# A list scheduler with other durations, a model of the TensorE clock, and due times shifted by kind in five stretches

## The chip, the cores and the metric

The kernel runs on one core of one Trainium2 chip. The metric is the device time of one execution in microseconds (us). The core has five engines with a queue each: TensorE (PE in the profile; its weight loads are PEld), VectorE (DVE), ScalarE (ACT), GpSimd (POOL) and SyncE (SP), which issues most DMAs.

## The reference

Two layers, one after the other, in float32. The first is a linear attention with a decaying state (4 batches, 8 heads, 768 steps, head size 48); the second a feed-forward net whose hidden layer is the maximum of three products. Cut to what matters:

```python
for t in range(S):                                   # S = 768
    cur = einsum('bhd,bhe->bhde', u[None] * k_t, v_t)
    y[:, :, t] = einsum('bhd,bhde->bhe', r_t, state + cur)
    state = w[None, :, :, None] * state + einsum('bhd,bhe->bhde', k_t, v_t)
x = y.transpose(0, 2, 1, 3).reshape(B * S, H * D)    # 3072 tokens x 384
h = maximum(maximum(x @ w1, x @ w2), x @ w3)         # 3072 x 768
out = h @ w_out                                      # 3072 x 384
```

## The kernel before

**Tiling.** The 768 steps are cut into 12 chunks of 64. A chunk holds 64 steps of 4 batches, that is 256 tokens, and each chunk is worked in two halves q of four heads. Within a chunk the recurrence is turned into matrix products: scores of r against k, a mask that keeps earlier steps, scores against v, and r against the state that earlier chunks left. Products are made from pairs of float16 numbers (a high and a low part) in three matmuls; chunk 0 uses float32 matmuls instead.

**Pieces of one chunk.** Loads from DRAM of `feat` (k and r, steps along the free dimension) and `tok` (k, r, v, steps along partitions). DVE or, from chunk 3, POOL scales them by powers of the decay (`kT`, `rT`, `kdec`) and makes the diagonal (`am`). ACT makes high parts (`kdh`, `rh`, `ah`, `ktdh`, `vdh`, `sdh`), DVE low parts (`kdl`, `rl`, `al`, `ktdl`, `vdl`, `sdl`). SP then copies kd, ktd, vd and sd block by block into kb, ktb, vb and sb by DMAs within the chip (`spread`, lines 308 to 310, two DMAs each). PE does `sc` (24 matmuls a half), `va` (48) and `ke` (24); `ke` leads to the next state. ACT and DVE take `va` out of PSUM as `xh` and `xl` (lines 456 and 461), the inputs of the feed-forward part. There PE does 18 `up` products of 9 matmuls each; the maximum is taken as they leave PSUM (ACT `m` at line 502, then DVE `m` twice at line 506); `hh` (ACT) and `hl` (POOL or DVE) are the parts of the result; three `dn` products of 18 matmuls give the output, which ACT takes out (`io`) and stores. ACT also sums squares of all inputs, of the state, of x and of the weights (`sq`, `xsq`, `wsq`; "junk" at lines 252 and 340), which DVE tests at the end (`check`, `good`, `flag`); the fallback behind the test isn't taken here.

**Weights** come once, in 16 pieces (`word`), as 64-bit numbers that ACT and DVE turn into float16 pairs: `ztop` (ACT), `word` (DVE), `his` (ACT), `lo` (DVE). Four buffers hold pieces that are under way.

**Order.** Nothing is ordered by hand line by line. A planner in the kernel's own Python (`Plan`, line 40) gets each piece with an engine, an expected duration, what it reads and writes, the buffers it takes and a due time in units of chunks. `order` (line 86) plays the pieces forward: of the pieces that could start first on an engine it takes the one with the smallest due time. The instructions are then written in the order of the planned starts, so every engine and the SP queue work through a fixed list, in order, and wait at its head whatever stands behind. A plan's times are never used on the chip, only its order.

**Due times.** Each piece's due time is its chunk plus an offset, plus a shift looked up by kind, such as `"act sq"`. Before, a kind has two shifts: one for due times up to `OPENING` = 1.6 and one behind. A transfer is expected to take its bytes by `RATE`, in one pipe, 1.5 us behind its issue, and to be seen 0.9 us after it ends. Kinds that stand next to GpSimd work are stretched (`near`). PE's pieces have one duration whatever its clock; chunk 0's are written at a slow clock (3.65 us for its `sc`).

Of the kernel before, what the change touches and what calls it, by code (L numbers as in the profile page):

```python
# [38 lines left out]

class Plan:  # L40

    LAG = {"pe": 0.25, "dve": 0.1, "act": 0.2, "pool": 0.15}
    ISSUE = {"sp": 0.45, "act": 0.45, "pool": 1.0}
    RATE, BEFORE, BEHIND = 275e3, 1.5, 0.9
    OPENING = 1.6
    SHIFT = {
        "act ah": (-5.31, -0.9), "act am": (2.08, 0), "act hh": (1.37, 0.4), "act his": (-0.69, 0), "act io": (-5.36, -2.55),
        "act kb": (-1.33, 0), "act kdh": (-2.9, 1.2), "act ktb": (1.56, 0), "act ktdh": (2.65, 0.45), "act m": (0.81, -0.9),  # L50
        "act odd": (0, 0.6), "act rh": (1.04, -0.85), "act sdh": (-5.26, 2.75), "act sq": (-6.83, 0.2), "act state": (-3.36, 0),
        "act tkt": (-0.31, 0), "act vb": (-2.77, 0), "act vdh": (-3.65, 2.05), "act xh": (1.12, -1.45), "act ztop": (-4.35, 0),
        "dve a": (4.95, 2.4), "dve al": (5.58, 0.7), "dve am": (-3.84, 0.85), "dve ends": (0, 0.45), "dve flag": (0, -2),
        "dve good": (0, -3), "dve hl": (2.63, -2.25), "dve kT": (6.29, 0), "dve kdec": (8.61, 0), "dve kdl": (-1.52, -0.15),
        "dve ktdl": (-3.55, 1.1), "dve lo": (-4.52, 0), "dve m": (-2.24, 0.3), "dve rT": (9.32, 0), "dve rl": (-2.27, 0.75),
        "dve sdl": (3.31, -0.15), "dve state": (-2.75, 1.5), "dve vdl": (4.98, 0.55), "dve vet": (0, -0.15), "dve word": (-1.81, 0),
# [10 lines left out]
    def do(self, due, eng, cost, fn, reads=(), writes=(), takes=(), size=0, near=0):  # L67
# [16 lines left out]
        self.todo.append(dict(n=n, due=due, eng=eng, cost=cost, fn=fn, need=need, takes=takes, size=size, near=near, kind=kind, late=late, touch={*reads, *writes, *new}))  # L84

    def order(self, free):

        free, pipe = dict(free), 0.0
# [14 lines left out]
        def earliest(p):  # L103
            t = free[p["eng"]]
            for m in p["need"]:
                q = self.todo[m]
                t = max(t, end[m] if q["eng"] != p["eng"] or q["size"] and not p["size"] else start[m] + busy[m] + (0 if p["size"] else 0.06))
# [7 lines left out]
            return t  # L115

        while ready:
# [30 lines left out]
        self.when = start  # L148
        return [self.todo[n] for n in sorted(out, key=lambda n: start[n])]
# [3 lines left out]
def kernel(ctx, tc, feat, tok, wu, ut, ws, wo, cst, out):  # L153
# [518 lines left out]
    def dma(due, fn, size, reads=(), writes=(), takes=(), eng="sp", n=1):  # L672
        do(due, eng, n * Plan.ISSUE[eng], fn, reads, writes, takes, size)
# [34 lines left out]
    def before_scores(c, q, due):
# [7 lines left out]
        dma(due - 0.22, lambda: spread(nc.sync, kb, kd, C), 524288, reads=["kdh", "kdl"], writes=["kb"], n=2)  # L716
# [13 lines left out]
    def before_keys(c, q, due):  # L730
# [5 lines left out]
        dma(due - 0.20, lambda: spread(nc.sync, ktb, ktd, C), 524288, reads=["ktdh", "ktdl"], writes=["ktb"], n=2)  # L736

    def before_values(c, q, due):
# [3 lines left out]
        dma(due - 0.22, lambda: spread(nc.sync, vb[q], vd[q], D), 393216, reads=[vh, vl], writes=[("vb", q)], n=2)  # L742

    def first_scores(q, due):
# [6 lines left out]
        do(due, "pe", 3.65, lambda: full("sc", q, kb, C, P, units(raws[c, q]["rT"])), reads=[f, "kb", ("rT", c, q)], takes=[("psa", ("sc", c, q))])  # L751
        do(due + 0.02, "dve", dve(U * C), lambda: mask(c, q), reads=[("sc", c, q)], writes=[("am", c, q)])

    def first_values(q, due):
        c = 0
        do(due, "pe", 2.8, lambda: full("va", q, vb[q], C, R, raws[c, q]["a"]), reads=[("am", c, q), ("vb", q)], writes=[("xq", 0)] * q, takes=[("psa", ("va", c, q))])
        leave_x(c, q, due)

    def first_keys(q, due):
# [3 lines left out]
        do(due, "pe", 3.2, lambda: full("ke", q, ktb, D, C + D, units(raws[c, q]["v"])), reads=["ktb", t], takes=[("psa", ("ke", c, q))])  # L763
# [13 lines left out]
    def after_keys(c, q, due):  # L777
# [17 lines left out]
    def leave_x(c, q, due):  # L795
# [12 lines left out]
        if q:  # L808
            do(due + 0.9, "act", act(NJ * TOK) + 0.1, lambda: x_sum(c, T["x", c][0]), reads=[hi], writes=[("xsq", c)])
# [19 lines left out]
    def ffn(c):  # L829
# [30 lines left out]
        def part(m, fs, due):  # L860
# [14 lines left out]
    do(-0.55, "pe", 1.1, turn, takes=[("psa", "turned")])  # L875
# [5 lines left out]
    do(-0.45, "pe", 2.2, stir, reads=[("xq", 0)], writes=["stirred"], takes=[("psm", "stir")])  # L881
# [15 lines left out]
    do(4.9, "dve", 1.2, check_ends, reads=[("begun", 4)], writes=["ends"])  # L897
    do(NCH - 0.4, "dve", 1.5, check, reads=["ends", *(k for k in plan.wrote if k[0] in ("sq", "xsq", "wsq"))], writes=["good"])
# [67 lines left out]
```

## Time and profile before

| | |
|---|---|
| median of 3 runs | 405.27 us (403.41, 405.27, 408.9) |
| the profiled execution's own time | 405.38 us |
| its span, first to last instruction | 403.5 us |
| mean granted TensorE clock | 0.983 |
| busy PE, PEld, DVE, ACT, POOL | 372.7, 334.0, 276.7, 265.1, 182.2 us |
| moved by DMA | 80.69 MB, mean 200 GB/s |

An engine's busy time is the time in which it executed something; ends of matmuls are modelled, so that a busy PE may still run at half its clock. A row of instructions gives its start, its length, engine, line, operation, out<-in, shapes, how many it merges, and in brackets the idle time before it with who ended it. SPq and ACTq are queues that issue DMAs.

### The profile page before, as it was taken

How to read it: one execution, taken by the hardware profiler on the slowest of the kernel's cores; microseconds unless marked ns; L12 is line 12 of the kernel's file. 1: busy time of each engine (PE TensorE's matmuls, PEld its weight loads, DVE VectorE, ACT ScalarE, POOL GpSimd, SP SyncE). 2: the span in 40 equal slices, each digit the busy share in tenths (PEclk: the TensorE clock that was granted, in tenths of full speed). 3: DMA queues.
4: the chain of work that ended last, by engine and by line, in shares of the span. 5: the costliest groups of instructions: out<-in, count | busy, mean ns of one | idle time of the engine just before them, and what ended most of it. 6: DMA issues, size and time to landing. Idle time of an engine off the chain costs nothing.

```text
span 403.5 us, 11979 instructions
## 1 busy us (share of the span) xinstructions
PE 372.7 (92%) x4768; PEld 334.0 (83%) x4768; DVE 276.7 (69%) x540; ACT 265.1 (66%) x698; POOL 182.2 (45%) x180
## 2 busy tenths in 40 slices
PE   2879788998999799999899999999999999999995
PEld 2877677887888589989789989999899989999784
DVE  6889889974859786695766865875876865443420
ACT  5989979695747755764764854765766784844421
POOL 9100000059655579658268378368557633010110
PEclk9998899999999789999999999999999999999999
DMA  8899787999399999859588688788887963500001
GB/s 288 310 326 257 200 238 213 280 286 263 107 247 244 292 264 255 214 166 255 138 262 232 151 247 240 191 216 217 235 209 202 268 162 88 147 2 15 27 2 45
DMA packets 28655, 80.69 MB, mean 200 GB/s; under 512 B 4528, under 2 KB 9392, under 8 KB 28592
## 3 DMA queue, kind: packets, MB, share of 16 engines
q1 hardware_dynamic: 23264, 75.03, 67.4%
q10 hardware_dynamic: 5328, 4.82, 3.8%
q8 instruction: 39, 0.64, 0.7%
q14 instruction: 24, 0.20, 0.2%
HBM read 36.41 MB, written 4.72 MB: 102 GB/s over the span
## 4 chain that ended last, share of the span: by engine, by line
PE 43%; DMA 16%; ACT 8%; DVE 6%; issue 3%; ACTq 1%; SPq 1%; POOL 0%; DVEq 0%
PE psm L487 36%; PE psa L400 7%; DMA kb<-kd 6%; DMA tok<-in_tok_dram 4%; DMA feat<-in_feat_dram 3%; DMA ktb<-ktd 3%; ACT xh L456 2%; ACT junk L340 1%; ACTq L867 1%; ACT junk L252 1%; DVE m L506 1%; DVE ktd L327 1%; ACT kd L322 1%; ACT rh L362 1%; ACT io L532 1%
## 5 line engine op out<-in xcount | busy, mean ns | idle before, releaser
L487 PEld LDWEIGHTS <-w 128*128 128x128 f16 x2592 | 252.2, 99 | 45.3 <-issue 14.4
L487 PE MATMUL psm<-xh,w 128*128 128x256 f16 x1296 | 226.3, 276 | 5.4 <-ACT m L502 2.7
L487 PE MATMUL psm<-xl,w 128*128 128x256 f16 x648 | 156.1, 276 | 5.3 <-DVE xl L461 4.9
L515 POOL TENSOR_TENSOR hl<-m,hh 128x256 f16<-128x256 f32 x55 | 45.6, 830 | 148.5 <-ACT hh L509 74.6
L506 DVE SCALAR_TENSOR_TENSOR m<-psm,m 128x256 f32<-128x256 f32 x144 | 60.1, 419 | 63.8 <-PE psm L487 37.5
L509 ACT CAST hh<-m 128x256 f16<-128x256 f32 x72 | 28.8, 401 | 64.0 <-DVE m L506 63.4
L487 PE MATMUL psm<-hh,w 128*128 128x256 f16 x432 | 55.7, 273 | 0.0
L357 POOL TENSOR_TENSOR feat<-feat,wrt 128x512 f32<-128x512 f32 x36 | 50.2, 1409 | 4.4 <-DMA feat<-in_feat_dram 4.4
L340 ACT ACTIVATE junk<-tok 128x384 bf16<-128x384 f32 x72 | 37.3, 518 | 14.5 <-DMA tok<-in_tok_dram 13.0
L376 POOL TENSOR_TENSOR am<-tok,u_sb 128x384 f32<-128x384 f32 x18 | 21.3, 1183 | 46.5 <-DVE al L420 32.6
L461 DVE SCALAR_TENSOR_TENSOR xl<-psa,xh 32x256 f16<-32x256 f32 (+2 forms) x60 | 28.2, 471 | 16.3 <-ACT xh L456 15.2
L502 ACT ACTIVATE m<-psm 128x256 f32<-128x256 f32 x72 | 27.1, 378 | 14.2 <-PE psm L487 10.5
L487 PE MATMUL psm<-hl,w 128*128 128x256 f16 x216 | 33.5, 273 | 0.7 <-POOL hl L515 0.7
L400 PE MATMUL psa<-ah,vb 128*128 128x64 f16 x352 | 33.9, 195 | 0.0
L400 PE MATMUL psa<-rh,sb 128*128 128x64 f16 x352 | 33.5, 195 | 0.0
L400 PE MATMUL psa<-al,vb 128*128 128x64 f16 x176 | 31.7, 195 | 0.6 <-DVE al L420 0.6
L400 PE MATMUL psa<-rl,sb 128*128 128x64 f16 x176 | 31.7, 195 | 0.0
L400 PEld LDWEIGHTS <-vb 128*128 128x128 f16 x528 | 29.8, 100 | 1.4 <-issue 0.8
L327 DVE TENSOR_TENSOR kd<-feat,kd 128x512 f16<-128x512 f32 x22 | 20.8, 944 | 13.1 <-ACT kd L322 12.6
L400 PEld LDWEIGHTS <-sb 128*128 128x128 f16 x528 | 28.1, 99 | 0.0
L456 ACT ACTIVATE xh<-psa 32x256 f16<-32x256 f32 (+2 forms) x60 | 24.9, 414 | 2.0 <-PE psa L400 1.2
L390 POOL TENSOR_TENSOR am<-cs,a 128x512 f32<-128x512 f32 x18 | 21.1, 1174 | 7.2 <-DVE a L381 7.2
(96 smaller groups left out, 550.0 us busy)
## 6 DMA issues: line engine op xcount, KB each, us to landing
tok<-in_tok_dram SPq DMA_DIRECT2D x24, 576.0 KB, 6.9
feat<-in_feat_dram SPq DMA_DIRECT2D x24, 512.0 KB, 5.3
raw<-in_ws_dram SPq DMA_DIRECT2D x12, 576.0 KB, 7.5
kb<-kd SPq DMA_DIRECT2D x22, 256.0 KB, 5.8
kb<-kd SPq DMA_DIRECT2D x22, 248.0 KB, 6.2
ktb<-ktd SPq DMA_DIRECT2D x20, 256.0 KB, 3.4
ktb<-ktd SPq DMA_DIRECT2D x20, 248.0 KB, 4.2
out_dram<-io ACTq DMA_DIRECT2D x36, 128.0 KB, 5.0
```

Of the source, the lines that this page charges most:

```text
L327: nc.vector.tensor_tensor(out=dense.dense[:, 1, :, 0:w], in0=src, in1=dense.dense[:, 0, :, 0:w], op=ALU.subtract)
L340: nc.scalar.activation(out=junk[:, 0:U * D].rearrange("p (u d) -> p u d", u=U), in_=src, func=AF.Square, scale=scale, accum_out=stat[:, ki ...
L357: helper(c).tensor_tensor(out=t[n], in0=t[n], in1=tb, op=ALU.mult)
L376: helper(c).tensor_tensor(out=w.rearrange("p (g b) d -> p g b d", g=2), in0=t["r"], in1=by_token(u_sb, q), op=ALU.mult)
L400: nc.tensor.matmul(out=ps, lhsT=l[i], rhs=rr[j], start=first and n == 0, stop=last and n == 2)
L456: nc.scalar.mul(out=hi, in_=src, mul=SC_X)
L461: nc.vector.scalar_tensor_tensor(out=lo, in0=src, scalar=SC_X, in1=hi, op0=ALU.mult, op1=ALU.subtract)
L487: nc.tensor.matmul(out=ps, lhsT=a, rhs=b, start=first and n == 0, stop=last and n == len(prods) - 1)
L502: nc.scalar.mul(out=m, in_=ps, mul=by)
L506: nc.vector.scalar_tensor_tensor(out=m, in0=ps, scalar=by, in1=m, op0=ALU.mult, op1=ALU.max)
L509: nc.scalar.copy(out=h[0][:, f, :], in_=m)
L515: lows_by(c, f).tensor_tensor(out=h[1][:, f, :], in0=m, in1=h[0][:, f, :], op=ALU.subtract)
```

## The change

The arithmetic, the tiles, the buffers and the number of instructions stay as they are. Only the plan's order changes, through four edits: a model of PE's clock in windows of 3.413 us (half speed until a window was busy for more than 88%, back to half when one was busy for less than 40%), with PE's durations given at full speed; new durations for some pieces; transfers given in us each in place of bytes by a rate; and a table of shifts with five values for each kind, for due times below 0, from 0, from 1, from 2 and from 10. Ties go to the piece that was made first. Cut to its core:

```diff
+class Clock:
+    WINDOW = 3.413
+    def __init__(self, phase):
+        self.began, self.fast, self.busy = phase - self.WINDOW, False, 0.0
+    def roll(self, t):
+        while self.began + self.WINDOW <= t:
+            share = self.busy / self.WINDOW
+            self.fast = share >= 0.4 if self.fast else share > 0.88
+            self.busy = 0.0
+            self.began += self.WINDOW
...
-    RATE, BEFORE, BEHIND = 275e3, 1.5, 0.9
-    OPENING = 1.6
+    BEFORE, BEHIND, PHASE = 1.5, 0.9, 1.4
+    CLASSES = (0.0, 1.0, 2.0, 10.0)
     SHIFT = {
-        "act sq": (-6.83, 0.2), "act xh": (1.12, -1.45), "act sdh": (-5.26, 2.75), "act ktdh": (2.65, 0.45),
-        "act kb": (-1.33, 0), "act rh": (1.04, -0.85), "pe up": (-0.67, 0), "pe va": (-2.94, -0.15),
-        "pe ke": (-1.11, 0.1), "pe sc": (-5.56, -0.3), "pe dn": (-9.56, 0.1), "dve ends": (0, 0.45),
-        "dve good": (0, -3), "pe count": (0, -1.9),
...
+        "act sq": (-1.7, 0.58, 15.04, 25.18, 3.62), "act xh": (14.36, -0.7, -1.17, 16.78, -3.76),
+        "act sdh": (0, -3.69, -7.86, -4.53, 0), "act ktdh": (23.8, -0.44, -2.39, -0.94, 0),
+        "act kb": (42.97, 0, 0, 0, 0), "act rh": (0.11, -2.53, -6.32, 19.43, -0.86),
+        "pe up": (0, -1.13, -3.38, -7.37, 3.91), "pe va": (-0.24, 0.81, 0, -2.99, 1.71),
+        "pe ke": (0, 1.99, 0.68, -0.01, 0), "pe sc": (0.87, 7.39, 0.34, -7.33, 1.81),
+        "pe dn": (0, -20.75, 9.7, -0.26, 0.34), "dve ends": (0, 0, 0, 0.61, 0),
+        "dve good": (0, 0, 0, 0, 2.99), "pe count": (0, 0, 0, 0, 5.95),
...
-        late = due > self.OPENING
-        due += self.SHIFT.get(kind, (0, 0))[late]
+        stage = sum(due >= x for x in self.CLASSES)
+        due += self.SHIFT.get(kind, (0,) * 5)[stage]
...
-            start[n], free[e] = t, t + cost
+            free[e] = clock.run(t, cost) if e == "pe" else t + cost
-                pipe = max(pipe, t + p["cost"] + self.BEFORE) + p["size"] / self.RATE
+                pipe = max(pipe, t + p["cost"] + self.BEFORE) + p["move"]
...
-        do(due - 0.05, "act", act(HN), lambda: tops(h, T[w]), ...)          # act(HN) = 0.59
+        do(due - 0.05, "act", 0.7, lambda: tops(h, T[w]), ...)
-    ... "act", act(U * D) + 0.1, ... square_sum(...)                         # 0.53
+    ... "act", 0.62, ... square_sum(...)
-    do(4.9, "dve", 1.2, check_ends, ...)
+    do(4.9, "dve", 1.6, check_ends, ...)
-    do(NCH - 0.4, "dve", 1.5, check, ...)
+    do(NCH - 0.4, "dve", 3.4, check, ...)
```

The other durations: `sc`, `va` and `ke` of chunk 0 from 3.65, 2.8 and 3.2 to 1.83, 1.4 and 1.6 us at full speed; `wsq` 0.69 to 0.79, `xsq` 0.85 to 0.97. The transfers, from the bytes by 275 kB/us to:

| transfer | before | after |
|---|---|---|
| feat | 1.91 | 1.45 |
| tok | 2.14 | 1.9 |
| word | 2.14 | 1.45 |
| kb, ktb | 1.91 | 2.1 |
| vb, sb | 1.43 | 1.5 |
| out | 0.48 | 0.4 |

More of the change, by code (lines that the diff above doesn't have):

```diff
@@ L37, with run @@
 SC_O = 1.0 / (X16 * W16 * W16 * H16)
+class Clock:
[8 more added lines that the diff above has]
+            self.began += self.WINDOW
+    def run(self, t, work):
+        self.roll(t)
+        while work > 1e-9:
+            end, speed = self.began + self.WINDOW, 1.0 if self.fast else 0.5
+            took = work / speed
+            if t + took <= end + 1e-12:
+                self.busy += took
+                return t + took
+            self.busy += end - t
+            work -= (end - t) * speed
+            t = end
+            self.roll(t)
+        return t
@@ L40 @@
 class Plan:
+    ENGINES = ("pe", "dve", "act", "pool", "sp")
     LAG = {"pe": 0.25, "dve": 0.1, "act": 0.2, "pool": 0.15}
     ISSUE = {"sp": 0.45, "act": 0.45, "pool": 1.0}
-    RATE, BEFORE, BEHIND = 275e3, 1.5, 0.9
-    OPENING = 1.6
+    BEFORE, BEHIND, PHASE = 1.5, 0.9, 1.4
+    CLASSES = (0.0, 1.0, 2.0, 10.0)
     SHIFT = {
[L49 to L56, printed above, removed]
[5 rows of a table removed]
@@ new lines @@
+        "sp feat": (-0.15, 0.96, 3.7, -3.35, 0),
+        "sp tok": (0.33, 1.42, -11.02, -2.55, 0),
+        "pe turned": (-3.43, 0, 0, 0, 0),
+        "act tkt": (-0.34, 0, 0, 0, 0),
+        "dve kT": (-8.93, 0.65, -2.23, 0, 0),
+        "act kb": (42.97, 0, 0, 0, 0),
+        "dve rT": (-0.48, 18.75, 1.61, 0, 0),
+        "act vb": (0.64, 0, 0, 0, 0),
+        "dve am": (-0.61, 24.67, 0.86, 0.89, 0.13),
+        "dve a": (-0.11, 0.51, -1.49, 5.05, -0.96),
+        "act sq": (-1.7, 0.58, 15.04, 25.18, 3.62),
@@ new lines @@
+        "pe sc": (0.87, 7.39, 0.34, -7.33, 1.81),
+        "pe va": (-0.24, 0.81, 0, -2.99, 1.71),
+        "act xh": (14.36, -0.7, -1.17, 16.78, -3.76),
+        "dve xl": (-0.37, -0.86, -0.13, -5.22, -0.75),
+        "act xsq": (0, 1.37, -7.66, -5.22, 0.61),
+        "pe stir": (-1.33, 0, 0, 0, 0),
+        "sp word": (-1.39, 2.21, 0, 0, 0),
+        "act ztop": (-1.21, 0.81, 0, 0, 0),
+        "dve word": (1.91, 1.76, 0, 0, 0),
+        "act his": (11.93, 21.35, 0, 0, 0),
+        "dve lo": (-0.07, -3.88, 0, 0, 0),
@@ new lines @@
+        "dve kdec": (2.44, 4.71, 2.04, 0, 0),
+        "act ktb": (0, 16.01, 0, 0, 0),
+        "pe ke": (0, 1.99, 0.68, -0.01, 0),
+        "act state": (0, 0.44, 0, 0, 0),
+        "act sdh": (0, -3.69, -7.86, -4.53, 0),
+        "dve sdl": (0, 29.98, 0.02, 6.1, 0),
+        "sp sb": (0, 0.96, 1.51, -3.12, 0),
+        "act kdh": (1.36, 1.21, 5.08, 3.18, 0.75),
+        "dve kdl": (-0.33, -0.48, -3.03, -0.14, 0),
+        "sp kb": (0, -0.13, 2.06, -0.53, 3.31),
+        "act rh": (0.11, -2.53, -6.32, 19.43, -0.86),
@@ new lines @@
+        "dve rl": (-0.25, -1.51, 0.03, -4.62, 2.93),
+        "act am": (0, 30.25, 33.68, 0, 0),
+        "act ah": (0, -0.17, -10.84, -0.38, -3.74),
+        "dve al": (0, -7, 3.78, -4.7, -0.86),
+        "act ktdh": (23.8, -0.44, -2.39, -0.94, 0),
+        "dve ktdl": (-3.71, 30.71, 1.97, 0, 0),
+        "sp ktb": (-4.63, 3.35, -0.97, 6.13, 0),
+        "act vdh": (0, -0.49, 3.27, -0.43, 17.94),
+        "dve vdl": (0, 3.34, 51.05, 1.01, 1.46),
+        "sp vb": (0, 1.49, 1.35, 0.52, -3.43),
@@ L62 @@
+        "pool am": (0, 0, -5.56, 0.53, 6.56),
+        "pool kdec": (0, 0, -0.43, 0.19, 0),
+        "act wsq": (0, 0, 0, -0.35, 0.68),
+        "dve ends": (0, 0, 0, 0.61, 0),
+        "dve good": (0, 0, 0, 0, 2.99),
+        "pe count": (0, 0, 0, 0, 5.95),
+        "dve flag": (0, 0, 0, 0, 1.59),
     }
@@ L65, in __init__, with do @@
         self.bufs, self.todo, self.wrote, self.read = bufs, [], {}, {}
-    def do(self, due, eng, cost, fn, reads=(), writes=(), takes=(), size=0, near=0):
+    def do(self, due, eng, cost, fn, reads=(), writes=(), takes=(), move=0, near=0):
         n = len(self.todo)
@@ L83, in do @@
         need.discard(n)
-        self.todo.append(dict(n=n, due=due, eng=eng, cost=cost, fn=fn, need=need, takes=takes, size=size, near=near, kind=kind, late=late, touch={*reads, *writes, *new}))
+        self.todo.append(dict(n=n, due=due, eng=eng, cost=cost, fn=fn, need=need, takes=takes, move=move, near=near, kind=kind, stage=stage, base=base, touch={*reads, *writes, *new}))
     def order(self, free):
-        free, pipe = dict(free), 0.0
+        free, pipe, clock = dict(free), 0.0, Clock(self.PHASE)
         left = {}
@@ L106, in earliest @@
                 q = self.todo[m]
-                t = max(t, end[m] if q["eng"] != p["eng"] or q["size"] and not p["size"] else start[m] + busy[m] + (0 if p["size"] else 0.06))
+                t = max(t, end[m] if q["eng"] != p["eng"] or q["move"] and not p["move"] else start[m] + busy[m] + (0 if p["move"] else 0.06))
             for pool, _ in p["takes"]:
@@ L115, in earliest, with first @@
             return t
+        def first(some):
+            return min(some, key=lambda m: (self.todo[m]["due"], m))
         while ready:
@@ L121, in order @@
             t = min(when.values())
-            n = min((m for m in when if when[m] <= t + 0.02), key=lambda m: self.todo[m]["due"])
+            n = first(m for m in when if when[m] <= t + 0.02)
             e = self.todo[n]["eng"]
-            n = min((m for m in when if self.todo[m]["eng"] == e and when[m] <= when[n] + 0.02), key=lambda m: self.todo[m]["due"])
+            n = first(m for m in when if self.todo[m]["eng"] == e and when[m] <= when[n] + 0.02)
             p, t = self.todo[n], when[n]
@@ L129, in order @@
                 cost += min(p["near"] * cost, p["near"] / (1 + p["near"]) * (free["pool"] - t))
-            start[n], free[e] = t, t + cost
-            busy[n] = cost
-            if p["size"]:
-                pipe = max(pipe, t + p["cost"] + self.BEFORE) + p["size"] / self.RATE
+            start[n] = t
+            free[e] = clock.run(t, cost) if e == "pe" else t + cost
+            busy[n] = free[e] - t
+            if p["move"]:
+                pipe = max(pipe, t + p["cost"] + self.BEFORE) + p["move"]
                 end[n] = pipe + self.BEHIND
             else:
-                end[n] = t + cost + self.LAG[e]
+                end[n] = free[e] + self.LAG[e]
             for pool, k in p["takes"]:
@@ L670, with dma @@
     do_tile = T.__setitem__
-    def dma(due, fn, size, reads=(), writes=(), takes=(), eng="sp", n=1):
-        do(due, eng, n * Plan.ISSUE[eng], fn, reads, writes, takes, size)
+    def dma(due, fn, move, reads=(), writes=(), takes=(), eng="sp", n=1):
+        do(due, eng, n * Plan.ISSUE[eng], fn, reads, writes, takes, move)
     def helping(c, columns):
@@ L696, in again @@
     def again(n, h, due):
-        do(due + 0.5, "act", act(HN) + 0.1, lambda: weight_sum(n, h), reads=[("his", n, h), ("begun", int(due))], writes=[("wsq", n, h)])
+        do(due + 0.5, "act", 0.79, lambda: weight_sum(n, h), reads=[("his", n, h), ("begun", int(due))], writes=[("wsq", n, h)])
     def fetched(c, q, due, behind=()):
-        dma(due, lambda: load_feat(c, q), 524288, reads=behind, writes=["fetched"], takes=[("feat", ("feat", c, q))])
-        dma(due, lambda: load_tok(c, q), 589824, reads=behind, writes=["fetched"], takes=[("tok", ("tok", c, q))])
+        dma(due, lambda: load_feat(c, q), 1.45, reads=behind, writes=["fetched"], takes=[("feat", ("feat", c, q))])
+        dma(due, lambda: load_tok(c, q), 1.9, reads=behind, writes=["fetched"], takes=[("tok", ("tok", c, q))])
     def squares(c, q, due):
@@ L750, in first_scores @@
         before_mask(c, q, due)
-        do(due, "pe", 3.65, lambda: full("sc", q, kb, C, P, units(raws[c, q]["rT"])), reads=[f, "kb", ("rT", c, q)], takes=[("psa", ("sc", c, q))])
+        do(due, "pe", 1.83, lambda: full("sc", q, kb, C, P, units(raws[c, q]["rT"])), reads=[f, "kb", ("rT", c, q)], takes=[("psa", ("sc", c, q))])
         do(due + 0.02, "dve", dve(U * C), lambda: mask(c, q), reads=[("sc", c, q)], writes=[("am", c, q)])
@@ L755, in first_values @@
         c = 0
-        do(due, "pe", 2.8, lambda: full("va", q, vb[q], C, R, raws[c, q]["a"]), reads=[("am", c, q), ("vb", q)], writes=[("xq", 0)] * q, takes=[("psa", ("va", c, q))])
+        do(due, "pe", 1.4, lambda: full("va", q, vb[q], C, R, raws[c, q]["a"]), reads=[("am", c, q), ("vb", q)], writes=[("xq", 0)] * q, takes=[("psa", ("va", c, q))])
         leave_x(c, q, due)
@@ L762, in first_keys @@
         do(due - 0.24, "act", 1.05, lambda: apart(ktb, units(raws[c, q]["k"]), C), reads=[t, ("kdec", c, q)], writes=["ktb"])
-        do(due, "pe", 3.2, lambda: full("ke", q, ktb, D, C + D, units(raws[c, q]["v"])), reads=["ktb", t], takes=[("psa", ("ke", c, q))])
+        do(due, "pe", 1.6, lambda: full("ke", q, ktb, D, C + D, units(raws[c, q]["v"])), reads=["ktb", t], takes=[("psa", ("ke", c, q))])
         after_keys(c, q, due)
@@ L874 @@
         fetched(0, q, -3 + 0.1 * q)
-    do(-0.55, "pe", 1.1, turn, takes=[("psa", "turned")])
+    do(-0.55, "pe", 0.55, turn, takes=[("psa", "turned")])
     do(-0.54, "act", 0.7, turned_back, reads=["turned"], writes=["tkt"])
```

39 lines of the change are left out of this document (26 added, 13 removed), and 5 rows, old and new, of the table SHIFT.

## Prediction

> **What bounds the kernel now.** I read the busy times first, then the stages, then in each stage what PE waited for.
>
> ```profile
> PE 372.7 (92%) x4768; PEld 334.0 (83%) x4768; DVE 276.7 (69%) x540; ACT 265.1 (66%) x698; POOL 182.2 (45%) x180
> ...
> core 0: us, PE busy (x) PEld busy (x) DVE busy (x) ACT busy (x) POOL busy (x), PEclk, DMA share, GB/s
> 0.00:30.00 30.00, 19.10 (x95) 17.42 (x96) 23.62 (x49) 23.76 (x54) 10.56 (x19) 1.00 0.85 307
> 30.00:60.00 30.00, 26.09 (x328) 22.59 (x328) 26.25 (x50) 26.60 (x67) 0.00 (x0) 0.89 0.87 234
> 60.00:110.00 50.00, 45.97 (x566) 40.06 (x566) 41.02 (x80) 39.16 (x108) 22.03 (x20) 1.00 0.81 230
> 110.00:150.00 40.00, 36.07 (x528) 31.10 (x526) 29.66 (x51) 25.32 (x69) 22.87 (x23) 0.91 1.01 262
> 150.00:370.00 220.00, 217.87 (x3010) 198.56 (x3007) 146.54 (x280) 140.78 (x379) 123.44 (x114) 1.00 0.70 189
> 370.00:403.50 33.50, 27.61 (x253) 24.25 (x250) 9.57 (x34) 9.48 (x26) 3.35 (x5) 0.99 0.08 27
> ```
>
> PE is the bound from 150 us on: there it idles 220 - 217.87 = 2.1 us, and an order can give no more back. The loss lies ahead of that: idle 10.9 us in the first 30, 3.9 in the next 30, 4.0 to 110 and 3.9 to 150. To that comes the slow clock, (1 - 0.89) x 30 = 3.3 us and (1 - 0.91) x 40 = 3.6 us. The last stage idles 5.9 us.
>
> What PE has to do at full clock is seen in the chain:
>
> ```profile
> 208.12 0.60 PE psa L400 x24
> ...
> 209.71 0.70 PE psa L400 x24
> ...
> 250.65 2.70 PE psa L400 x96
> 253.35 10.81 PE psm L487 x99
> ```
>
> An up or dn matmul takes 10.81 / 99 = 0.109 us, and the 2,592 of them 283 us; ke 0.60, sc 0.70, and va the 1.4 that are left of 2.70: 2 x 11 x 2.7 less two ke of chunk 11 is 58 us. With some 10 us for chunk 0's float32 matmuls at full clock (six groups, of which one quoted below takes 3.67 us at half) and 5 us from the last matmul to the end (398.52, below), PE needs 356 of 403.5 us, loads ahead of its first matmul not counted. Nearly all that is open lies before 150 us.
>
> Two stalls there tell how they are lost. The first:
>
> ```profile
> 94.84 0.59 SPq L310 DMA_DIRECT2D kb<-kd  x1
> 106.39 0.46 SPq L309 DMA_DIRECT2D sb<-sd  x1
> ...
> 110.53 0.58 SPq L181 DMA_DIRECT2D tok<-in_tok_dram  x1
> ...
> 98.52 0.52 ACT L340 ACTIVATE junk<-tok 128x384 bf16<-128x384 f32 x1 [4.57 <-DMA tok<-in_tok_dram]
> 99.69 1.54 ACT L456 ACTIVATE xh<-psa 96x256 f16<-96x256 f32 x4
> ...
> 101.26 1.76 DVE L461 SCALAR_TENSOR_TENSOR xl<-psa,xh 96x256 f16<-96x256 f32 x4 [5.18 <-ACT xh L456]
> ...
> 100.00:110.00 10.00, 8.94 (x115) 7.47 (x113) 8.53 (x17) 7.92 (x22) 7.26 (x7) 1.00 0.34 98
> ...
> ACT junk L340 <- DMA tok<-in_tok_dram: 13.0, 9, 4.6
> ```
>
> A sum of squares, which nobody needs before the end, stands at the head of ACT's queue and waits 4.57 us for its `tok`. Behind it stand xh, and then the state's parts; DVE waits for xh, and SP, also in order, issues nothing from 95.4 to 106.39. So the DMAs run at a share of 0.34 for 10 us, and at 1.01 for the 40 us behind: the hole is paid there. Squares wait so nine times, 13.0 us in all.
>
> The second is the clock:
>
> ```profile
> 33.44 0.42 PE L487 MATMUL psm<-xh,w 128*128 128x256 f16 x1
> 33.65 0.42 PE L487 MATMUL psm<-xl,w 128*128 128x256 f16 x1
> ...
> 36.03 0.27 PE L487 MATMUL psm<-xh,w 128*128 128x256 f16 x1
> 36.14 0.27 PE L487 MATMUL psm<-xl,w 128*128 128x256 f16 x1
> ...
> 44.28 0.27 PE L487 MATMUL psm<-xh,w 128*128 128x256 f16 x1 [2.48 <-ACT m L502]
> 44.89 0.42 PE L487 MATMUL psm<-xl,w 128*128 128x256 f16 x1
> 45.10 0.85 PE L487 MATMUL psm<-xh,w 128*128 128x256 f16 x3
> ...
> 48.24 0.27 PE L487 MATMUL psm<-xh,w 128*128 128x256 f16 x1
> ...
> 134.01 0.52 ACT L322 ACTIVATE sd<-state 128x384 f16<-128x384 f32 x1 [0.86 <-DMA ktb<-ktd]
> ...
> 134.85 1.54 ACT L456 ACTIVATE xh<-psa 96x256 f16<-96x256 f32 x4
> ...
> 137.66 0.37 PE L487 MATMUL psm<-xl,w 128*128 128x256 f16 x1 [1.74 <-DVE xl L461]
> ```
>
> Matmuls start 0.21 us apart before some 34 us and 0.11 behind. After a wait of 2.48 us the 0.21 comes back at 44.7 and lasts until 48.2, 3.4 us. The same happens after the wait that ends at 137.66: there xh stood behind a state piece that waited for a DMA.
>
> **The change part by part.** It neither adds nor removes an instruction; what moves is the order. I work out places by hand from due times, and what each could give from the stage's loss. Where only the plan's run would tell the new order, the term is bounded: at best the stage's whole loss, at worst the same amount added.
>
> *Squares.* For the second half of chunk 3 they are due at 2.40 and 2.80 (at + 0.5 q + 0.05 - 0.15, + 0.4). Before, 0.2 is added: among the first on ACT. After, 25.18: last of all that is ready; for due times from 1 to 2, 15.04 in place of -6.83 or 0.2. A piece placed last is placed later than its data, so that a late `tok` finds it less often at the head. The cover that pays is ACT's idle time: 220 - 140.78 us behind 150. What it may cost is one of the three tok buffers, held longer. This takes away the first stall and with it the hole: of 4.0 us to 110 I take 2, of 3.9 + 3.6 to 150 I take 5, since the wait that drops the clock at 137 is a consequence of late transfers too.
>
> *The clock model* counts a window as lost if PE idles in it. From 30 to 60 us ACT and DVE are busy 26.60 and 26.25 of 30, so the order can only choose what waits: of 3.9 + 3.3 I take 2.5.
>
> [...]
>
> *The opening.*
>
> ```profile
> 29.19 0.27 PE L487 MATMUL psm<-xh,w 128*128 128x256 f16 x1 [1.06 <-ACT xh L456]
> ...
> 10.20 0.69 DVE L357 TENSOR_TENSOR feat<-feat,wrt 128x512 f32<-128x512 f32 x1
> ...
> 10.74 0.52 ACT L340 ACTIVATE junk<-tok 128x384 bf16<-128x384 f32 x1
> ...
> 14.83 1.26 ACT L467 ACTIVATE kb<-feat 64x512 f32<-64x512 f32 x2
> ...
> 16.14 3.67 PE L473 MATMUL psa<-feat,kb 128*128 128x64 f32 x16 [0.21 <-ACT kb L467]
> ```
>
> kb's second half could start at 10.9 and starts at 14.83, behind squares and a weight; PE waits for it. After, kb has 42.97 added and goes last, but squares of this stage still go early (-1.7) and wait for a `tok` that lands behind `feat`, so kb may slip in ahead. SP's first ten DMAs keep their order: loads are chained to each other, and four weights fill their buffers. I take 1.5 of 10.9; the bounds are -3.9 (kb as late again) and 3.9.
>
> *From 150 on.*
>
> ```profile
> 172.56 1.20 DVE L541 TENSOR_TENSOR ends<-ends,bt 128x4 f32<-128x4 f32 x1
> 173.79 1.20 DVE L539 TENSOR_SCALAR bt<-wu_sb 128x4 f32<-128x4 f32 x1
> ...
> 380.51 0.19 PE L563 MATMUL psa<-good,ones 128*1 128x1 f32 x2 [0.87 <-DVE good L559]
> ...
> 398.52 0.38 ACT L532 ACTIVATE io<-psm 128x256 f32<-128x256 f32 x1 [1.05 <-PE psm L487]
> ```
>
> Two of the six instructions of the test of the ends take DVE 1.20 us each; the plan had 1.2 us for all six and has 1.6, still short. I take 1 of 2.1. PE's wait of 0.87 us for the final test may go as its count moves to the end (5.95 for -1.9): 0.5. The last store's tail stays.
>
> Sum: 1.5 + 2.5 + 2 + 5 + 1 + 0.5 = 12.5 us. Against the profiled execution's 405.38 (its span and 1.9 us around it; the median is 405.27, the same) that is **393 us**. With all that the terms could give (3.9 + 7.2 + 4.0 + 7.5 + 2.1 + 0.9 = 25.6) it would be 380.
>
> **The rivals.**
>
> *Stalls only move* (0.20). Loads at full share move 307 / 0.85 = 361 GB/s, so a word of 590 kB takes 1.63 us and not the new 1.45. By the table of durations a chunk's transfers are 22.3 us in the plan (22.9 before); its 5.9 MB of loads and copies and 0.39 MB of output, by the sizes in the code, take 24 at the 262 GB/s of 110 to 150 us. The plan is still hopeful where the DMAs are the bound, and another piece (vdh, or POOL's products of tok) heads a queue in place of the squares. Then of the 9.5 us between 30 and 150 only 2 come, beside the 3 of the other stages: 405.4 - 5 = 400. For it: the share of 1.01; against: it was as hopeful before, and the squares are what waited 13.0 us.
>
> *The clock isn't where the plan has it* (0.08). Of my terms about 3.5 us are clock; if they fail and two more windows of 3.4 us run at half, at 1.7 us each, the time is 393 + 6.9 = 400. [...]
>
> *The stalls keep their places* (0.06): the order changes in pieces that don't matter, 405.
>
> *xh comes too late* (0.13): slower. For due times from 2 to 10, xh has 16.78 added (before -1.45): of ACT's pieces only squares and rh still rank behind it. x is handed over while PE does ke, sc and dn: 0.60 + 0.70 + 54 x 0.109 = 7.2 us; xh and xl need 1.54 + 1.76. So 3.9 us are spare, some eight ACT pieces of 0.5 us. Beyond them each 1 us costs PE 1 us in every chunk of 3 to 10. In the stall above xl waited 5.18 us: 1.5 more than there is, over eight chunks, is 12 us, and with 3 us kept of the other terms 414. Against it: ACT is busy only 64% of that stage.
>
> **How the numbers follow.** A measurement of this kernel tells 2%, 8.1 us, from no change: below 397.2 is faster, above 413.4 slower. The forecast of 393 has 0.53, nearly all of it faster, with a range of its own from 383 to 400; the 400 and 405 cases together 0.34, with some 0.04 that end below 397; the slower one 0.13. So faster 0.56, same 0.31, slower 0.13. The range reaches from 381, the whole of the terms, to 409, with the 405 case inside and most of the slower one out.
>
> **What would show it.** Squares: no wait of ACT's squares for `tok` over 2 us, no slice with DMA share under 0.5 before 150, PE's busy time from 60 to 150 above 85 of 90 us. Clock: fewer than three stretches at 0.21 us behind 30 us. Opening: the first up matmul before 29.19, and kb's second half by 12. From 150: PE's idle time under 1 us in 200. Wrong would be: PE waiting for xl in every chunk behind 150, or for words in the first 60 us because the weights' chain (`his` has 11.93 and 21.35 added) goes last on a full ACT.

## The result, and the profile after

The changed kernel takes **425.19 us** (four runs, 421.83 to 426.85) against 405.39 us of the kernel before in four runs beside it (403.41 to 408.9): a ratio of 1.0468, with an interval of 1.0368 to 1.0567. It is slower by some 20 us where I had forecast 12 us faster. The profiled execution took 426.24 us, its span is 424.5 us and its mean granted clock 0.965.

The busy times of the page and the stages of the changed kernel (us; busy time and instructions of PE, PEld, DVE, ACT and POOL; granted clock, DMA share, GB/s):

```profile
PE 378.7 (89%) x4768; PEld 339.3 (80%) x4768; DVE 283.9 (67%) x540; ACT 264.6 (62%) x698; POOL 186.9 (44%) x180
...
0.00:30.00 30.00, 19.84 (x101) 18.33 (x101) 24.63 (x50) 24.05 (x54) 10.56 (x19) 1.00 0.79 278
30.00:60.00 30.00, 24.23 (x280) 20.87 (x281) 24.46 (x45) 25.18 (x62) 0.00 (x0) 1.00 0.95 267
60.00:110.00 50.00, 45.28 (x587) 40.04 (x585) 41.72 (x81) 37.92 (x109) 17.04 (x16) 0.90 0.85 243
110.00:150.00 40.00, 35.77 (x465) 31.95 (x464) 26.53 (x46) 24.45 (x69) 24.85 (x21) 0.99 0.82 224
150.00:200.00 50.00, 47.64 (x644) 42.31 (x643) 32.10 (x63) 27.02 (x73) 30.03 (x29) 0.94 0.59 161
200.00:250.00 50.00, 43.97 (x583) 39.22 (x580) 32.08 (x56) 27.88 (x76) 26.30 (x23) 0.97 0.76 207
250.00:300.00 50.00, 48.27 (x675) 43.44 (x675) 34.34 (x61) 29.09 (x79) 32.45 (x31) 0.97 0.66 176
```

The loss is not where I looked. PE's busy time up to 60 us differs little in sum, and at the first `up` of chunk 3 the kernel is only 3.0 us behind (138.6 against 135.6 us). From 150 to 300 us, where PE had idled 1.8 us, it now idles 2.4 + 6.0 + 1.7 = 10.1 us, and its clock is below 1. The same stages before:

```profile
150.00:200.00 50.00, 48.49 (x664) 44.12 (x661) 35.77 (x72) 32.23 (x87) 32.49 (x29) 1.00 0.81 210
200.00:250.00 50.00, 49.68 (x667) 45.02 (x665) 35.01 (x64) 29.73 (x82) 34.10 (x32) 1.00 0.80 223
250.00:300.00 50.00, 50.00 (x745) 45.91 (x744) 36.23 (x66) 33.53 (x90) 31.38 (x28) 1.00 0.79 211
```

The groups of PE's instructions, with the idle time ahead of them and who ended it, say for what. First before (line 487), then after (line 569):

```profile
L487 PE MATMUL psm<-xh,w 128*128 128x256 f16 x1296 | 226.3, 276 | 5.4 <-ACT m L502 2.7
L487 PE MATMUL psm<-xl,w 128*128 128x256 f16 x648 | 156.1, 276 | 5.3 <-DVE xl L461 4.9
...
L569 PE MATMUL psm<-xh,w 128*128 128x256 f16 x1296 | 226.6, 278 | 21.5 <-ACT m L584 19.7
L569 PE MATMUL psm<-xl,w 128*128 128x256 f16 x648 | 158.0, 279 | 0.4 <-DVE xl L543 0.4
```

PE waits 19.7 us for ACT's `m`, which takes products out of PSUM, and waited 2.7 before; for `xl`, my slower rival, it waits 0.4 us, and waited 4.9 before. ACT is busy 62% of the span. So what did it do instead? Its rows around one of these waits:

```profile
140.64 0.38 ACT L584 ACTIVATE m<-psm 128x256 f32<-128x256 f32 x1
140.92 0.38 ACT L614 ACTIVATE io<-psm 128x256 f32<-128x256 f32 x1
146.15 0.34 ACTq L949 DMA_DIRECT2D out_dram<-io  x1
146.54 0.52 ACT L422 ACTIVATE junk<-tok 128x384 bf16<-128x384 f32 x1 [5.24 <-DMA kb<-kd]
...
148.35 0.51 ACT L404 ACTIVATE sd<-state 128x384 f16<-128x384 f32 x1
148.76 0.36 ACT L584 ACTIVATE m<-psm 128x256 f32<-128x256 f32 x1
```

`io`, the last third of a chunk's output, is ready at 141.30, but its store is issued at 146.15, 4.86 us later, and everything behind it in ACT's queue stands still. The bracket of the next row names who ended it: a DMA of kd into kb, which has nothing to do with the output. The chain of work through the same place tells it in order (start, length, what):

```profile
137.60 8.48 DMA kb<-kd
146.07 0.02 issue
146.10 0.02 ACTq L949
...
146.15 0.34 ACTq L949
...
148.45 0.41 ACT sd L404
148.86 0.28 ACT m L584
149.14 0.04 issue
149.18 2.93 PE psm L569 x13
```

Why does a store wait for a copy? In the traces before and after, each of the kernel's 275 DMAs raises one of eight semaphores (100, 102, 103, 104, 106 to 109) when it lands, a semaphore being here a counter that a DMA raises and an issue waits for. The eight are handed out in turn over both queues. An issue that gets a number again first waits until the DMA before with that number has landed: the short row at 146.10 is the store's wait, for number 107. So at most eight are in flight, and by issues and landings eight is the most in both profiles. The trace's semaphore events for this place, put in a table:

| issue, us | queue | what | semaphore | landed, us |
|---|---|---|---|---|
| 136.91 | SP | sb | 106 | 144.61 |
| 137.60 | SP | **kb** | **107** | **146.07** |
| 138.18 | SP | kb | 109 | 147.00 |
| 140.35 | SP | feat | 102 | 148.38 |
| 141.95 | SP | tok | 103 | 151.31 |
| 144.63 | SP | ktb | 106 | 153.20 |
| 146.15 | ACT | **third store** | **107** | 154.11 |
| 147.01 | SP | vb | 109 | 154.47 |

Each issue with a used number follows the landing: 144.61 and 144.63, 146.07 and 146.15, 147.00 and 147.01. In SP's queue only further DMAs stand behind such a wait. In ACT's, in order, it holds up `m`, `hh`, the state's parts and the squares. The profile's sizes of the eight in flight behind the issue of `feat` at 140.35 (feat 512 KB, tok 576, sb 192 and 186, kb 256 and 248, two stores of 128) make 2.2 MB. At this stage's 224 GB/s they would take 10 us, an estimate of how late a DMA can be when its number is wanted again; the `kb` here took 8.5 us from issue to landing.

In the changed kernel the third store of chunks 2 to 8, which goes out while PE is already in the `up` products of the next chunk, waits 4.86, 3.68, 4.86, 4.13, 2.77, 4.46 and 5.26 us. In the kernel before the same wait was there in six of these seven, at 0.47 to 1.19 us, and its chain had shown it:

```profile
229.19 3.89 DMA feat<-in_feat_dram
...
233.16 0.34 ACTq L867
...
233.60 0.39 ACT m L502
```

A load of `feat` is followed by a store that doesn't read `feat`. This row I had before me and passed over.

### The profile page after: what moved, and what is told of

Read it like the earlier page. It is cut to its first block, busy times and chain, and to the rows that moved or that the text cites. A ratio compares the mean times of both kernels' runs of the same rounds, so it can differ in the third digit from the quotient of the medians.

```text
span 424.5 us, 12020 instructions
## 1 busy us (share of the span) xinstructions
PE 378.7 (89%) x4768; PEld 339.3 (80%) x4768; DVE 283.9 (67%) x540; ACT 264.6 (62%) x698; POOL 186.9 (44%) x180
## 4 chain that ended last, share of the span: by engine, by line
PE 50%; DMA 25%; ACT 8%; DVE 6%; issue 4%; ACTq 1%; SPq 0%; DVEq 0%
PE psm L569 41%; DMA kb<-kd 12%; PE psa L482 9%; DMA vb<-vd 4%; DMA raw<-in_ws_dram 3%; DMA sb<-sd 2%; DMA raw<-in_wo_dram 2%; ACT junk L422 2%; DMA ktb<-ktd 2%; DVE vd L411 1%; ACT io L614 1%; DVE w L330 1%; ACT junk L334 1%; DVE state L518 1%; ACT xh L538 1%
## 5 line engine op out<-in xcount | busy, mean ns | idle before, releaser
L569 PEld LDWEIGHTS <-w 128*128 128x128 f16 x2592 | 255.1, 100 | 57.6 <-issue 24.2
L569 PE MATMUL psm<-xh,w 128*128 128x256 f16 x1296 | 226.6, 278 | 21.5 <-ACT m L584 19.7
L569 PE MATMUL psm<-xl,w 128*128 128x256 f16 x648 | 158.0, 279 | 0.4 <-DVE xl L543 0.4
L439 POOL TENSOR_TENSOR feat<-feat,wrt 128x512 f32<-128x512 f32 x36 | 48.5, 1351 | 101.2 <-DVE am L459 69.0
L597 POOL TENSOR_TENSOR hl<-m,hh 128x256 f16<-128x256 f32 x55 | 41.8, 761 | 49.4 <-ACT hh L591 49.4
L569 PE MATMUL psm<-hh,w 128*128 128x256 f16 x432 | 58.0, 279 | 0.0
L422 ACT ACTIVATE junk<-tok 128x384 bf16<-128x384 f32 x72 | 37.5, 520 | 29.2 <-DMA kb<-kd 27.1
L411 DVE SCALAR_TENSOR_TENSOR sd<-state,sd 128x384 f16<-128x384 f32 x22 | 20.8, 944 | 31.5 <-ACT sd L404 26.1
L569 PE MATMUL psm<-hl,w 128*128 128x256 f16 x216 | 33.9, 276 | 0.0
L459 POOL TENSOR_TENSOR am<-am,tok 128x384 f32<-128x384 f32 x18 | 29.4, 1633 | 1.4
```

The source lines that it names most:

```text
L411: nc.vector.scalar_tensor_tensor(out=dense.dense[:, 1, :, 0:w], in0=src, scalar=scale, in1=dense.dense[:, 0, :, 0:w], op0=ALU.mult, op1=AL ...
L422: nc.scalar.activation(out=junk[:, 0:U * D].rearrange("p (u d) -> p u d", u=U), in_=src, func=AF.Square, scale=scale, accum_out=stat[:, ki ...
L439: helper(c).tensor_tensor(out=t[n], in0=t[n], in1=tb, op=ALU.mult)
L459: helper(c).tensor_tensor(out=w, in0=w, in1=units(t["k"]), op=ALU.mult)
L569: nc.tensor.matmul(out=ps, lhsT=a, rhs=b, start=first and n == 0, stop=last and n == len(prods) - 1)
L597: lows_by(c, f).tensor_tensor(out=h[1][:, f, :], in0=m, in1=h[0][:, f, :], op=ALU.subtract)
```

## The experiments

The theory, *eight*: the whole loss is this wait in ACT's queue, some 18 us of PE's idle time and four windows at half clock behind it. The rivals: the new **model** (durations, transfers, clock) gives a bad order whatever the table; the final **test**, now last, lengthens the end; the **order** of ACT's pieces is at fault and not the limit. Ratios are to the kernel before, run on the same chip, with 95% intervals.

### Stores from SP

All output stores of the changed kernel are issued from SP, with the order unchanged; and the same edit on the kernel before.

```diff
-            nc.scalar.dma_start(out=out[m, :, ...
+            nc.sync.dma_start(out=out[m, :, ...
```

> The changed kernel, with its plan and order untouched, but the 36 output stores are issued from SyncE's queue in place of ScalarE's. Theory 'eight': a DMA's issue waits until the DMA issued eight before it has landed, and the third store of a chunk holds ScalarE's queue for 3 to 5 us that way; PE's six long waits for ScalarE's m (18.4 us in all) and the four slow-clock windows behind them (4 x 1.7) go: about 400 us. Rival 'late transfers': loads that come in bursts make all transfers late, and PE will wait for kb, ktb or sb instead: 418 or more. Rival 'xh too late' (from the prediction): nothing changes, 425.

Measured: 403.06 us, 0.9954 (0.9925 to 0.9982). The stages that had lost most:

```profile
150.00:200.00 50.00, 48.23 (x727) 44.17 (x726) 38.58 (x71) 32.25 (x86) 27.50 (x24) 1.00 0.74 195
200.00:250.00 50.00, 49.28 (x684) 44.63 (x682) 34.89 (x62) 29.21 (x81) 33.66 (x32) 1.00 0.79 207
250.00:300.00 50.00, 49.69 (x651) 45.12 (x648) 36.10 (x65) 31.87 (x90) 34.92 (x31) 1.00 0.86 234
```

PE idles 2.8 us in 150 in place of 10.1, and the clock is whole. By the ratios some 21 us are back with one word of the code. The rival in the expectation, late transfers that PE would then wait for as copies, falls.

> The kernel before with the 36 output stores issued from SyncE's queue. Theory 'eight': there the third store waits about 1 us in six chunks and PE hardly feels it: 403 to 406 us, no change. If stores on ScalarE cost both kernels alike for another reason, it gains 10 us or more.

Measured: 407.43 us, 1.006 (1.0026 to 1.0095), above the 403 to 406 that I expected. Stores from SP as such bring nothing and here cost some 0.6%; they cure a block that the kernel before hardly has.

### Only the third store from SP

```diff
-            nc.scalar.dma_start(out=out[m, :, ...
+            (nc.sync if m == 2 else nc.scalar).dma_start(out=out[m, :, ...
```

> The changed kernel with only the third output store of each chunk (m = 2, 12 of 36) issued from SyncE. Theory 'eight' puts the whole loss on that store: 403 us, as with all 36 moved. If it is ScalarE's issuing of stores as such (36 times some 0.35 us and what stands behind), only a third of the 22 us comes back: about 418.

Measured: 401.48 us, 0.9863 (0.9811 to 0.9915). One store in three carries the whole loss. The other two don't cost time on ACT: with them left there the ratio is lower than with all on SP (0.9954).

### The old table in the new model

The changed planner, with the two shifts of before.

```diff
-        due += self.SHIFT.get(kind, (0,) * 5)[stage]
+        due += self.SHIFT.get(kind, (0, 0))[due > self.OPENING]     # SHIFT of before
```

> The changed planner (clock model, new durations and transfers) with the table of shifts and the two stretches of before. If the new table makes the burst of loads and the late stores: 400 to 410 us, stores waiting 1 us or less. If the new durations do: 418 to 428 us with third stores waiting 3 us or more.

Measured: 417.16 us, 1.0288 (1.0222 to 1.0355), which is neither of the two cases expected: the third stores wait at most 1.0 us, and yet it is slower. The loss lies ahead of chunk 2's first `up` (124.4 us, 101.4 before); behind it some of it comes back. It begins in rows like this one of PE:

```profile
38.88 0.37 PE L522 MATMUL psm<-xh,w 128*128 128x256 f16 x1 [8.38 <-ACT xh L491]
```

The first `up` starts at 38.9 us (29.2 before). So within the new model the recurring block needs the new table, and the old table doesn't fit the new model's opening. The new table in the old model wasn't run.

### The final test early

In the last stretch `good`, `count` and `flag` get back the early places.

```diff
-"dve good": (0, 0, 0, 0, 2.99), "pe count": (0, 0, 0, 0, 5.95), "dve flag": (0, 0, 0, 0, 1.59)
+"dve good": (0, 0, 0, 0, -3),   "pe count": (0, 0, 0, 0, -1.9), "dve flag": (0, 0, 0, 0, -2)
```

> The changed kernel with the last-stretch shifts of the final test (good, count, flag) as before: -3, -1.9, -2. The tail from the last dn matmul to the end was 7.8 us against 5.0, because every engine reads the flag and branches behind it: 422.4 us if that is the cause of the 2.8 us, 425 if not.

Measured: 423.41 us, 1.0468 (1.0401 to 1.0535): 1.8 us from the changed kernel's median, with the same ratio. From the last `dn` to the end it takes 6.8 us, against 7.8 in the changed kernel and 5.0 before. It is no large part of the loss; a gain isn't shown.

> The changed kernel with all stores issued from SyncE and the final test's shifts as before (good -3, count -1.9, flag -2). If both causes add: 403.1 less the 2.8 us of the tail, about 400.3, which would be 1.2% under the kernel before. If the tail isn't set by the flag: 403.

With the stores from SP as well: 401.33 us, 0.987 (0.9818 to 0.9922); 6.0 us at the end. The interval overlaps that of the stores alone.

### `io` early

ACT's `io` gets an early due time in stage 3; PE's and SP's orders stay line by line the same.

```diff
-"act io": (0, -2.94, -1.77, 3.71, -0.98),
+"act io": (0, -2.94, -1.77, -2.55, -0.98),
```

> The changed kernel with one number changed: the shift of io and its store for due times from 2 to 10 goes from 3.71 back to -2.55; PE's and SyncE's orders stay the same, line by line. If the store's late key makes the wait: 400 to 406. If it is the eight DMAs in flight at that place of SyncE's order, wherever on ScalarE the store stands in these microseconds: still blocked, 420 to 428.

Measured: 424.09 us, 1.0448 (1.0378 to 1.0518). The block stays: third stores wait 3.0 to 4.9 us. One of them, and ACT's waits in all:

```profile
138.20 0.38 ACT L614 ACTIVATE io<-psm 128x256 f32<-128x256 f32 x1
142.74 0.34 ACTq L949 DMA_DIRECT2D out_dram<-io  x1
143.12 0.38 ACT L584 ACTIVATE m<-psm 128x256 f32<-128x256 f32 x1 [4.55 <-DMA sb<-sd]
...
ACT m L584 <- DMA sb<-sd: 28.4, 7, 5.2
```

Now `m` itself stands behind the store, and a copy of sd is the DMA that had the store's number before. So the early or late key of `io` isn't the cause. The rival *order of ACT's pieces* falls only in this form: the limit makes the wait, and what ACT does between `io` and its store decides whether it hurts, as the next run shows.

### The planner knows of the eight

The rule goes into the plan: a transfer can't be issued ahead of the planned landing of the transfer eight before. Nothing else is touched.

```diff
+            if p["move"] and len(moves) >= 8:
+                t = max(t, end[moves[-8]])
...
+                moves.extend([n] * p["copies"])          # copies: DMAs that a piece issues
```

> The changed kernel with one rule more in its planner: a DMA can't be issued before the DMA eight before it has landed, by the plan's own times. Stores stay on ScalarE. If the blocked store is a thing that the plan only didn't know of, it puts other ScalarE work ahead of the store: 400 to 406. If the plan's landing times are too early by the microseconds that count, the store still blocks: 412 or more.

Measured: 400.32 us, 0.9864 (0.9811 to 0.9917), span 396.6, the shortest of all. Around a store ACT now reads:

```profile
134.22 0.39 ACT L617 ACTIVATE io<-psm 128x256 f32<-128x256 f32 x1 [0.51 <-PE psm L572]
...
136.99 0.36 ACT L587 ACTIVATE m<-psm 128x256 f32<-128x256 f32 x1
...
140.98 0.37 ACT L587 ACTIVATE m<-psm 128x256 f32<-128x256 f32 x1
...
144.60 0.38 ACT L587 ACTIVATE m<-psm 128x256 f32<-128x256 f32 x1 [0.37 <-PE psm L572]
146.06 0.40 ACT L594 CAST hh<-m 128x256 f16<-128x256 f32 x1 [1.07 <-DVE m L591]
146.93 0.34 ACTq L952 DMA_DIRECT2D out_dram<-io  x1
```

The store goes out 12.3 us after its `io`, and in that time ACT goes on with other pieces, busy 6.3 us of it. PE's waits are down to this:

```profile
PE psm L572 <- ACT m L587: 2.4, 4, 1.6
```

2.4 us for `m` in place of 19.7. The stores stay on ACT, and by the names of its tiles PE's order is that of the changed kernel, so this shows the cause from a second side. The rule moves SP's DMAs too; that it isn't a gain of its own is tested on the kernel before.

> The kernel before, its table and durations, with the planner's rule of eight. Its third stores wait about 1 us and PE hardly waits for them: 402 to 407. If the rule by itself is worth something, also for SyncE's own DMAs: below 400.

The same rule in the planner of before: 405.53 us, 1.0011 (0.995 to 1.0072). With the old table it finds next to nothing to repair.

> The changed kernel with the planner's rule of eight and with the final test's shifts as before (-3, -1.9, -2). If the tail's 2.8 us come on top: 397.5 to 398.5, a ratio near 0.98. If the flag's place is worth nothing: 400.

The rule and the early test: 402.36 us, 0.9919 (0.9873 to 0.9966). I expected less than with the rule alone and missed. From the last `dn` to the end it takes 5.0 us in place of 6.0, but the whole time didn't follow, so a gain isn't shown.

### Without the clock model

The last kernel, with PE always fast in the plan.

```diff
-            self.fast = share >= 0.4 if self.fast else share > 0.88
+            self.fast = True                                        # and True at the start
```

> The same, but the planner's clock always runs at full speed, with PE's durations for full speed. If the clock model orders the opening better: 401 or more, with more windows at half speed in the first 80 us. If it hardly matters for the order: 397 to 400.

Measured: 422.54 us, 1.0418 (1.035 to 1.0486), 20 us more. 7.8 us of it are there by the first `up`, and 19.3 by chunk 3's:

```profile
30.00:60.00 30.00, 18.88 (x189) 15.33 (x190) 23.61 (x43) 23.92 (x53) 0.00 (x0) 0.74 0.86 230
...
35.09 0.23 PE L485 MATMUL psa<-rh,kb 128*128 128x64 f16 x1 [8.61 <-DMA kb<-kd]
```

PE waits 8.61 us for kb, and the clock is at half from 28.8 to 45.8 us. From chunk 3 on a chunk takes 29 us again. This doesn't show that the clock model is right, only that these shifts and the model go together; without it the same shifts give another order.

### The squares alone

The kernel before, with the squares placed last behind the opening.

```diff
-        "act sq": (-6.83, 0.2),
+        "act sq": (-6.83, 25.18),
```

> The kernel before with one number changed: the shift of the squares for due times over 1.6 is 25.18 in place of 0.2, so that they go last on ScalarE from chunk 2's second half on. By the prediction's step (a square waiting 4.57 us at the head of ScalarE's queue makes the hole in the DMAs at 100 to 110 us, and that the waits to 150): 5 to 7 us less, 398 to 400. If the stall is only the place where a late load is felt first: 403 to 407.

Measured: a ratio of 0.9974 (0.9925 to 1.0022); the profiled execution took 407.39 us. No gain. ACT's waits, and its rows and SP's at the stall that I had quoted:

```profile
ACT junk L340 <- DMA tok<-in_tok_dram: 21.2, 15, 3.6
...
97.91 0.52 ACT L340 ACTIVATE junk<-tok 128x384 bf16<-128x384 f32 x1 [3.24 <-DMA tok<-in_tok_dram]
...
94.35 0.59 SPq L310 DMA_DIRECT2D kb<-kd  x1
106.26 0.46 SPq L309 DMA_DIRECT2D sb<-sd  x1
```

Squares now wait 15 times for `tok`, 21.2 us, where it was 9 times and 13.0 us, and SP's hole of 11 us stays. By its code the planner takes what could start first and never holds an engine back: placed last, a square still gets the next free slot of ACT as soon as the plan believes `tok` there. That the plan believes it too early is my reading of the waits; the plan's own times are not on record.

## Why the prediction was wrong

**The step that failed** is the term *From 150 on* of the sum, +1 us, and behind it the reading that PE idles only 2.1 us there, so that an order can give no more back. Of a loss in that stage I thought only in the rival on xh. I counted each issue in an in-order queue, and for SP what stands behind it, but not what an issue waits for. From chunk 4's first `up` to the last `dn` it takes 243.8 us in the changed kernel, 229.0 before and 227.1 with the rule (table below): in place of +1 the term came out at -14.8 us, and +1.9 with the rule. Over the whole kernel, by the ratios, a loss of 4.7% turns into a gain of 0.5% (stores from SP) or 1.4% (third store, the rule), that is 21 to 25 us of 405.

The rest of the working can be judged on the kernel with the rule. First `up` matmul of a chunk, and the end of the last `dn`, by the starts in the traces (us):

| | before | after | with the rule |
|---|---|---|---|
| chunk 0 | 29.2 | 33.1 | 31.8 |
| chunk 1 | 63.3 | 74.8 | 71.8 |
| chunk 2 | 101.4 | 108.6 | 105.0 |
| chunk 3 | 135.6 | 138.6 | 134.0 |
| chunk 4 | 169.5 | 172.9 | 163.5 |
| chunk 9 | 317.0 | 336.9 | 310.8 |
| last dn | 398.5 | 416.7 | 390.6 |
| from there to the end of the span | 5.0 | 7.8 | 6.0 |

- *Squares*, 2 + 5 us: the size of the second term is about right, its reason isn't shown. From chunk 3 to 4 it takes 29.5 us with the rule and 33.9 before, 4.4 us less, and the clock of 110 to 150 is whole; from 60 to 150 us PE is busy 85.6 us in place of 82.0. The step "A piece placed last is placed later than its data" fell with the squares alone. In the changed kernel squares wait only 1.0 us for `tok`, and 9.4 us with the rule, at most 1.4 at a time, where it was 13.0 and up to 4.57. So something else of the new order keeps them apart; which, I haven't separated.
- *Clock model*, 2.5 us between 30 and 60: wrong. PE's busy time there fell from 26.09 to 24.23 us. Half clock shows as `up` matmuls that start 0.21 us apart, in place of 0.11 at full clock. Before, there were two windows of it in this stage (31.1 to 34.5 and 44.7 to 48.2); now there is one, from the first `up` to 36.6, and three in the next stage (63.9 to 74.1, clock 0.90). The slice's own 1.00 misleads, since the record of the clock begins with its first change, at 36.56 us (rows below). With the rule it is no better: PE is busy 44.2 us in the first 60, 45.2 before.
- *Opening*, 1.5 us: PE's busy time in the first 30 us rose by 0.74 us, but the first `up` comes 3.9 us later, and kb's second half starts at 15.55 us, not ahead of 12. One new wait behind it is ACT's `ztop`, which waits 1.69 us for a word at 42.46 and holds up `m`: the chain of the weights that I had named.
- *The final test*, 0.5 us: PE's wait of 0.87 us for `good` is gone, as I said, but the end grew by 2.8 us. I hadn't asked what follows the test.
- *From 150 on*, 1 us: with the rule, 227.1 us from chunk 4's first `up` to the last `dn`, and 229.0 before: 1.9 us. The size is near once the block is away, but my sign for it, under 1 us of idle time in 200, isn't met: PE idles 1.9 us from 150 to 370 and idled 2.1 before. What the test of the ends gave isn't separated.

PE's rows of the changed kernel around 36.56 us, first at half clock and then at full:

```profile
36.06 0.42 PE L569 MATMUL psm<-xh,w 128*128 128x256 f16 x1
36.28 0.42 PE L569 MATMUL psm<-xl,w 128*128 128x256 f16 x1
...
37.30 0.27 PE L569 MATMUL psm<-xh,w 128*128 128x256 f16 x1
37.41 0.27 PE L569 MATMUL psm<-xl,w 128*128 128x256 f16 x1
```

So with the rule the change gains 1.6 us up to chunk 3, 4.4 in it, 1.9 behind it, and loses 1.0 at the end: 6.9 us of span. By the ratio it is 5.5 us, less than half of the 12.5 forecast. Two slips of the working change nothing here: all the terms together give 380, and the range starts from 381; and 5.18 us is 1.3 more than the 3.9 that are spare for xh, not 1.5.

**The rivals.** *Stalls only move* had the right kind, another piece at the head of an in-order queue, and for it I had even looked at how full the DMAs are. But it priced late loads ahead of 150 us at 400 us; a store that pays for all DMAs ahead of it, once a chunk, wasn't in it. *xh comes too late* had the right place, ACT's queue once a chunk, and the right direction, but the wrong piece: that it said slower is luck. *The clock* was a consequence: four half windows of 3.4 us, 4 x 1.7 = 6.8 us of the loss. Together with PE's waits for `m` in those chunks (18.4 us by the starts of matmuls) that makes 25 us, near the 21 to 25 that the runs give back.

## What to carry to other kernels

When an order changes, ask for each instruction that issues a DMA what that issue waits for, not only what its data wait for: here DMAs in flight were limited to eight, and an issue in a compute engine's queue held up that engine for up to 5.26 us, until an unrelated transfer had landed. In a chain of waits, a transfer followed by an instruction that doesn't read it was the sign here. A plan that lacks such a limit can be tuned into it; teaching the limit to the plan, or moving the one issue to a queue with no arithmetic behind it, was worth more here than shifting the key of the piece ahead of it.

## What the hardware did that I had not expected

**Eight DMAs in flight**, over both queues together, is what this kernel's semaphores allow; a ninth issue waited up to 5.26 us.

**Half clock came in whole windows, on one grid in each of the two profiles, and what a stall of PE cost here went by where it fell on that grid.** In the clock record before and after, every stretch at half (granted clock 0.50) lasts 3.41, 6.83 or 10.24 us, that is one, two or three times 3.413, but for the one that runs into the end. Four in the changed kernel's trace start at 149.2, 183.3, 217.5 and 251.6 us, each 34.1 us, ten times 3.413, behind the one before. With that grid, the share of a window in which PE was busy, from the starts of its matmuls:

| stall of PE, us | length | busy share of the window hit | next window |
|---|---|---|---|
| 145.5 to 149.2 | 3.7 | 0.01 | half |
| 179.8 to 182.4 | 2.5 | 0.29 | half |
| 213.0 to 216.7 | 3.7 | 0.23 | half |
| 247.3 to 250.3 | 3.0 | 0.38 | half |
| 280.9 to 282.5 | 1.6 | 0.60 | full |
| 311.5 to 314.8 | 3.3 | 0.55 and 0.48 | full |

A stall of 2.5 us was followed by half clock and one of 3.3 us, across two windows, was not. The border lies between 0.38 and 0.48 in these rows. By the same count the other falls to half clock ahead of the last `dn` came behind windows 0.34 busy (after, at 63.9 us) and 0.17, 0.23 and 0.37 (before, at 31.1, 44.7 and 136.9 us). All half stretches of one profile lie on one grid; from one profile to the other it moved: they start 0.37 us behind a multiple of 3.413 us in the profile of before and 2.43 in that after. The plan's threshold of 0.4 fits these rows; its one fixed phase of 1.4 us can't fit both profiles.
